# A Fourier, soft-expert and gated layer on one Trainium2 core: the first transform split over 48 rows on the array's quarters, and the row softmax of seven batches moved into the expert loop

## Chip, cores and metric

The kernel runs on one core of a Trainium2 chip. The time is the device time of the whole program in microseconds (us). PE is the matmul engine (TensorE), with its weight loads as PEld; DVE is VectorE, ACT ScalarE, POOL GpSimd, SP the engine that only issues DMAs. Each engine works through its own queue in order. A name with a q behind it (SPq, ACTq) is the queue itself.

## What is computed

```python
def reference(x, w_r, w_i, b_r, b_i, phi, w1, w2, w_gate, w_val, w_out):
    X = rfft(x, axis=1)                        # x: 8 batches, 3072 rows, 256 columns
    Y = soft((X.re + i X.im) @ (w_r + i w_i) + b_r + i b_i)    # shrunk by 0.01 on each part
    x = irfft(Y, n=3072, axis=1).reshape(24576, 256)
    logits = x @ phi                           # 32 slots, 4 for each of 8 experts
    d = softmax(logits, axis=0)                # over all 24576 rows: which rows fill a slot
    slot = relu(d.T @ x, per expert @ w1) @ w2 # 8 experts, 256 to 1024 to 256
    c = softmax(logits, axis=1)                # over the 32 slots of a row
    x = c @ slot
    return (silu(x @ w_gate) * (x @ w_val)) @ w_out            # 256 to 1536 to 256
```

All inputs are float32, the weights of the last layer float64.

## The kernel before

The program has two large parts with a short one between.

**The transform stage** (`phase1`) goes through the 8 batches. The transform of 3072 points is split as 96 x 32. `load_x` (L714) brings a quarter of a batch's columns as `[96, 32, 64]` (for batch 0 `load_first`, L700). `stage_a` (L729) multiplies it by the 96-point table `fwd`: 16 calls a batch, one float32 matmul of 96 rows, 128 outputs and 512 columns each, into one of two PSUM banks that carry the name "ac". VectorE transposes the bank into `chan` (L734). A float32 matmul shows as two records in the trace. `stage_c` (L751) does the 32-point part out of `chan`, also through the two "ac" banks; ScalarE and VectorE split its result into a high and a low part in `xg` and `sg`. `stage_b` (L846) multiplies by the weights, in banks of its own ("pb"), three matmuls to a product. The result is shrunk, collected in `yt`, multiplied by `phi` (`stage_q`, L944) and spread over the partitions by DMAs (L973). From there `logits`, `slots` and `combine` make the softmax over all rows, step by step over the batches, and the softmax over the slots.

`combine` works on a `[96, 32, 32]` tile of logits: maximum of each row (DVE), subtraction (POOL, L1307), exponential (ACT), then sum and reciprocal (`total`, DVE, L1316 to L1318), scaling (`scale`, POOL, L1321), transpose (`turn`, DVE, L1325), a high part (`hi`, ACT, L1330) and a low part (`lo`, POOL, L1334), and a store of both to `c_scr` in DRAM. For the last batch `total` to `store` run in the middle part.

The order of all instructions of this stage is written by a planner (`Plan`). Each job has an engine, a cost (`COST`), a rank and the buffers that it needs; the planner always takes the job that can start first, by rank among equals, and `SHIFT` moves the rank of each kind of job by a fitted number.

**The middle part** (`after_slots`) runs the 8 experts on the slots, loads c of batch 0 (`load_c(0)`, L1685, three DMAs of 384 KB on POOL's queue) and the last layer's weights, and makes the table `gstk` from the slots and the gate weights (`gates`, L1717 to L1720).

**The expert loop** (so called in the diff's words for the gated last layer) has 576 steps, 72 a batch. A step makes two products of c with `gstk` (`gv`, L1733 and L1734), the gate on ACT (L1736), their product on DVE (L1738), and a split into a high and a low part (`split`, ACT L1745, DVE L1746); `mm_out` (L1758) of the step three before then runs six matmuls of 128x128x512. Every 12 steps two banks are transposed by DVE and stored.

Of the kernel before, what the change touches and what calls it, by code (L numbers as in the profile page):

```python
# [10 lines left out]
F32 = mybir.dt.float32  # L11
# [12 lines left out]
R2 = 32  # L24
NCH = 24
# [7 lines left out]
def dft_tables():  # L33
# [7 lines left out]
    n1 = np.arange(R1)  # L41
    n2 = np.arange(R2)
    k2 = np.arange(R2)
    sign = np.where(k2 >= R2 // 2, -1.0, 1.0)
    alt1 = np.where(n1 % 2 == 0, 1.0, -1.0)
    alt2 = np.where(n2 % 2 == 0, 1.0, -1.0)
    k1 = np.array([[j, 23 + j] for j in range(NCH)])
    k1[0] = (0, 47)

    fwd = np.zeros((R1, 4, 32))  # L50
    mix = np.zeros((4, R2, NCH, 2, 2, R2))
    for j in range(NCH):
        for h in range(2):
            if j == 0 and h == 0:
                fwd[:, 0, 0] = 1.0
                fwd[:, 1, 0] = alt1
                for i in range(R2):
                    if i == 0:
                        mix[0, :, j, 0, h, 0] = 1.0
                        continue  # L60
                    src = 0 if i < 16 else 1
                    k = 96 * i if i < 16 else 48 + 96 * (i - 16)
                    a = 2 * np.pi * ((n2 * k) % n) / n
                    mix[src, :, j, 0, h, i] = np.cos(a)
                    mix[src, :, j, 1, h, i] = -np.sin(a)
                continue
            a = 2 * np.pi * ((n1 * k1[j, h]) % R1) / R1
            fwd[:, 2 * h, j] = np.cos(a)
            fwd[:, 2 * h + 1, j] = -np.sin(a)
            a = 2 * np.pi * ((n2[:, None] * (k1[j, h] + 96 * k2)[None, :]) % n) / n  # L70
            mix[2 * h, :, j, 0, h, :] = np.cos(a)
            mix[2 * h + 1, :, j, 0, h, :] = np.sin(a)
            mix[2 * h, :, j, 1, h, :] = -np.sin(a) * sign
            mix[2 * h + 1, :, j, 1, h, :] = np.cos(a) * sign
# [56 lines left out]
    last[0:32, 0] = alt2  # L131
# [3 lines left out]
    def pad(m, rows):  # L135
# [3 lines left out]

    small = np.concatenate(  # L140
        [
            pad(np.concatenate([np.zeros((R1, 8)), fwd.reshape(R1, 128)], 1), R1),
# [17 lines left out]
for _n, _w in (  # L160
# [11 lines left out]
FWD = 136  # L172
# [5 lines left out]
    "load_f": 2.81,  # L178
    "setup_small": -9.39,
    "load_first": -3.7,  # L180
    "stage_a.mm": -28.93,
    "stage_a.turn": 2.94,
    "put": -0.33,
    "free_early": -16.09,
    "load_w": -25.29,
    "mix_w": 3.51,
    "part_w": -17.96,
    "rest_w": -0.28,
    "stage_c.mm": (-12.22, -1.28, -5.52),
    "stage_c.hi": (53.77, -42.32, -55.05),  # L190
    "stage_c.lo": (40.1, 19.86, -25.02),
    "stage_c.one_part": (2.25, -2.27, 4.93),
    "stage_c.add_part": (-68.16, 19.01, -25.95),
    "stage_c.sum_hi": (10.97, 9.66, -13.31),
    "stage_c.sum_lo": (-6.92, -75.37, -42.83),
    "stage_c.last_mm": (36.23, 0.0, 0.0),
    "stage_c.last_out": (-24.98, 0.0, 0.0),
    "stage_b.last_mm": (-10.11, 0.0, 0.0),
    "stage_b.last_out": (3.76, 0.0, 0.0),
    "stage_b.mm": (-0.22, -0.26, -0.14),  # L200
    "after_b.take": (48.09, 1.97, 4.29),
    "after_b.gather": (-37.89, -92.44, -12.86),
    "after_b.relu": (21.51, 7.9, 2.96),
    "after_b.join": (-54.79, -9.98, 9.41),
    "stage_q.mm": (0.0, -9.39, 7.88),
    "stage_q.turn_y": (7.74, 49.03, -2.46),
    "stage_q.turn": (-12.53, -0.89, 4.91),
    "stage_q.spread": (-23.98, -39.91, 59.31),
    "logits.inv_mm": -18.3,
    "logits.sp_mm": -38.62,  # L210
    "logits.sp_out": 26.62,
    "logits.rot": 64.93,
    "logits.join": -32.12,
    "logits.turn": -71.72,
    "logits.l_mm": 44.13,
    "logits.colmax": -29.68,
    "logits.keep_l": 51.42,
    "logits.spread": 15.76,
    "logits.max_mm": 33.28,
    "logits.newmax": 26.07,  # L220
    "logits.factor": 18.59,
    "logits.bc_mm": -2.58,
    "logits.lower": -7.03,
    "logits.expo": -25.93,
    "slots.f_mm": -12.38,
    "slots.turn": 9.73,
    "slots.cross": -27.68,
    "slots.rot": -4.89,
    "slots.join": -8.33,
    "slots.d_mm": -36.49,  # L230
    "slots.evac": -14.41,
    "slots.slot_mm": -32.07,
    "slots.gather": -18.97,
    "combine.rowmax": 14.04,
    "combine.lower": 1.85,
    "combine.expo": -54.13,
    "combine.total": -16.96,
    "combine.scale": -4.82,
    "combine.turn": -12.43,
    "combine.hi": -27.19,  # L240
    "combine.lo": 7.86,
    "combine.store": -22.54,
    "narrow.load": 28.3,
    "narrow.bits": 1.55,
    "narrow.size": 21.04,
    "narrow.value": -7.49,
    "narrow.store": -31.84,
    "load_x": 0.13,
    "narrow.part": 9.87,
    "narrow.rest": 4.99,  # L250
    "stage_q.mm'": (0.0, 0.0, -7.18),
    "stage_q.turn_y'": (0.0, 0.0, 12.3),
    "stage_q.turn'": (0.0, 0.0, 11.0),
    "stage_q.spread'": (0.0, 0.0, -21.67),
    "logits.inv_mm'": -32.46,
    "logits.sp_mm'": -32.14,
    "logits.sp_out'": 25.91,
    "logits.rot'": 31.71,
    "logits.join'": -6.39,
    "logits.turn'": -6.55,  # L260
    "logits.l_mm'": -67.64,
    "logits.colmax'": 60.65,
    "logits.keep_l'": 33.35,
    "logits.spread'": 13.57,
    "logits.max_mm'": -18.0,
    "logits.newmax'": 9.47,
    "logits.factor'": 18.28,
    "logits.bc_mm'": 12.87,
    "logits.lower'": -25.45,
    "logits.expo'": 35.72,  # L270
    "slots.f_mm'": 59.73,
    "slots.turn'": 49.73,
    "slots.cross'": 30.87,
    "slots.rot'": -12.01,
    "slots.join'": 52.75,
    "slots.d_mm'": 12.44,
    "slots.evac'": -2.82,
    "slots.slot_mm'": -78.14,
    "slots.gather'": -22.49,
    "combine.rowmax'": 5.14,  # L280
    "combine.lower'": -35.75,
    "combine.expo'": -34.15,
    "combine.total'": 20.3,
    "combine.scale'": 53.34,
    "combine.turn'": 70.78,
    "combine.hi'": 5.94,
    "combine.lo'": -32.53,
    "combine.store'": 28.18,
    "free_x": -27.72,
    "free_a": 45.67,  # L290
    "free_b": 2.84,
    "fetch_w1": 13.94,
    "fetch_w2": -26.03,
    "fetch_wg": -14.12,
    "hold": 25.89,
# [8 lines left out]
    "stage_a.mm": {"PE": 0.865},  # L304
# [15 lines left out]
    "stage_q.mm": {"PE": 0.56},  # L320
    "stage_q.turn_y": {"DVE": 1.215},
    "stage_q.turn": {"DVE": 0.432},
    "logits.inv_mm": {"PE": 1.32},
# [58 lines left out]
class Plan:  # L382
# [6 lines left out]

    LAG = 0.07  # L390
    HAND, SET, SEEN = 0.65, 0.9, 0.65
    SHY = 0.18

    def __init__(self, shift):
        self.tasks = []
# [111 lines left out]
def kernel(  # L507
# [1084 lines left out]
    def after_slots(ypool, rest):  # L1592
# [65 lines left out]
        for job in rest[0]:  # L1658
            job()
# [162 lines left out]
```

## Time and profile before

| | us |
|---|---|
| median of 3 runs | 1739.52 (1737.23 to 1740.32) |
| the profiled execution: its own time | 1739.96 |
| its span, first to last instruction | 1738.2 |
| PE busy in the span | 1697.5 (98%) |
| VectorE busy | 1283.1 (74%) |
| ScalarE busy | 981.0 (56%) |
| GpSimd busy | 301.2 (17%) |

Busy times are read against the same engine's span. Idle time of an engine that is not the limit costs nothing. The granted clock is that of PE as a share of 2.4 GHz: 1.00 is 2.4 GHz, and a value between 0.5 and 1.00 means that part of the stretch ran at 1.2 GHz.

### The profile page before, as it was taken

The numbers are of one execution on the slowest core, as the hardware profiler recorded it, in microseconds if no ns is written. First come the engines' busy times: TensorE is split into PE (matmuls) and PEld (weight loads), VectorE is DVE, ScalarE is ACT, GpSimd is POOL, SyncE is SP. The second block draws the span as 40 slices with busy tenths as digits, with TensorE's granted clock in tenths as the row PEclk, the third lists the DMA queues.
The fourth block names the chain that finished last, engine by engine and source line by source line (L and its number), as shares of the span: only waits on it lengthen the run. The fifth ranks groups of instructions, "written<-read, shape, count | busy, mean of one in ns | idle before, by whom it ended". The sixth has DMA issues, their size and how long they took to land.

```text
span 1738.2 us, 23243 instructions
## 1 busy us (share of the span) xinstructions
PE 1697.5 (98%) x8266; PEld 1288.5 (74%) x8266; DVE 1283.1 (74%) x2114; ACT 981.0 (56%) x1809; POOL 301.2 (17%) x287
## 2 busy tenths in 40 slices
PE   7999999999999889999999999999999999999998
PEld 4667666676666657888888888888888888888886
DVE  5687978878887536777777777777777777777776
ACT  2565654656556325656656566565565665656654
POOL 1344544445455440000000000000000000000000
PEclk9999999999999999999999999999999999999999
DMA  9557565576545795113112112113112112111111
GB/s 186 97 123 134 128 140 107 138 124 143 136 94 167 232 304 95 25 25 52 24 20 48 23 25 53 25 25 52 25 25 52 25 25 52 25 25 25 25 25 25
DMA packets 258468, 134.44 MB, mean 77 GB/s; under 512 B 209232, under 2 KB 243760, under 8 KB 258352
## 3 DMA queue, kind: packets, MB, share of 16 engines
q1 hardware_dynamic: 248352, 110.14, 31.2%
q0 software_dynamic: 8304, 22.02, 5.5%
q8 instruction: 65, 1.06, 0.3%
q10 hardware_dynamic: 1696, 0.79, 0.2%
q14 instruction: 51, 0.42, 0.1%
HBM read 69.99 MB, written 37.75 MB: 62 GB/s over the span
## 4 chain that ended last, share of the span: by engine, by line
PE 85%; DVE 8%; ACT 2%; DMA 2%; issue 1%; SPq 1%; POOL 0%; DVEq 0%; ACTq 0%; POOLq 0%
PE o L1758 46%; PE pg L1733 8%; PE pb L846 8%; PE pv L1734 8%; PE ac L729 5%; PE ac L751 4%; PE ch L944 1%; PE ch L1015 1%; DVE yt L960 1%; PE ch L1217 1%; PE pb L1578 1%; DVE xg L773 1%; DVE cv L1372 1%; DVE chan L734 1%; DMA x<-in_x_dram 1%
## 5 line engine op out<-in xcount | busy, mean ns | idle before, releaser
L1758 PE MATMUL o<-hh,wo 128*128 128x512 f32 x2304 | 722.5, 395 | 0.0
L1738 DVE TENSOR_TENSOR h<-sg,pv 128x512 f32<-128x512 f32 x576 | 394.3, 685 | 275.5 <-ACT sg L1736 274.1
L1736 ACT ACTIVATE sg<-pg 128x512 f32<-128x512 f32 x576 | 344.6, 598 | 426.1 <-PE pg L1733 426.1
L1758 PEld LDWEIGHTS o<-hh,wo 128*128 128x128 f32 x2304 | 434.3, 188 | 100.7
L1758 PE MATMUL o<-hl,wo 128*128 128x512 f32 x1152 | 453.8, 394 | 0.0
L1746 DVE TENSOR_TENSOR hl<-h,hh 128x512 fp32r<-128x512 f32 x576 | 393.9, 684 | 0.1
L1745 ACT ACTIVATE hh<-h 128x512 fp32r<-128x512 f32 x576 | 359.4, 624 | 0.2 <-DVE h L1738 0.2
L1758 PEld LDWEIGHTS o<-hl,wo 128*128 128x128 f32 x1152 | 216.1, 188 | 51.9
L1733 PE MATMUL pg<-cst,gstk 96*128 96x512 f32 x576 | 228.9, 397 | 3.4 <-DMA cst<-c_scr 3.4
L1734 PE MATMUL pv<-cst,gstk 96*128 96x512 f32 x576 | 226.6, 393 | 0.7 <-DVE gstk L1720 0.7
L918 POOL TENSOR_TENSOR yt<-r,yt 128x512 f32<-128x512 f32 x96 | 126.6, 1319 | 207.4 <-ACT yt L909 121.8
L1685 POOL DMA_DIRECT2D cst<-c_scr x24 | 13.4, 565 | 803.4 <-PE pv L1734 797.4
L846 PE MATMUL pb<-xg,wh 128*128 128x512 f32 x384 | 140.6, 447 | 3.3 <-ACT yt L899 2.1
L1734 PEld LDWEIGHTS pv<-cst,gstk 96*128 96x128 f32 x576 | 110.0, 191 | 26.6 <-DVE gstk L1720 1.4
L1733 PEld LDWEIGHTS pg<-cst,gstk 96*128 96x128 f32 x576 | 108.3, 188 | 28.7 <-issue 4.6
L729 PE MATMUL ac<-xq,fwd 96*128 96x512 f32 x224 | 111.8, 612 | 3.9 <-DVE chan L734 3.4
L751 PEld LDWEIGHTS ac<-cm,chan 128*128 128x128 f32 x768 | 97.5, 196 | 15.7 <-issue 6.9
L734 DVE STREAM_TRANSPOSE chan<-ac 128x512 f32<-128x512 f32 x128 | 88.4, 702 | 25.7 <-PE ac L729 22.7
L751 PE MATMUL ac<-cm,chan 128*128 128x128 f32 x768 | 104.5, 286 | 1.7 <-DVE xg L773 1.3
L846 PEld LDWEIGHTS pb<-xg,wh 128*128 128x128 f32 x384 | 66.1, 189 | 41.9 <-issue 17.3
L770 ACT ACTIVATE xg<-ac 128x512 fp32r<-128x512 f32 x96 | 56.6, 595 | 47.5 <-PE ac L751 45.7
L792 POOL TENSOR_TENSOR sg<-sf,sg 128x256 fp32r<-128x256 f32 x96 | 70.2, 745 | 68.0 <-ACT sg L788 56.1
(145 smaller groups left out, 1590.0 us busy)
## 6 DMA issues: line engine op xcount, KB each, us to landing
out_dram<-ob SPq DMA_DIRECT2D x190, 128.0 KB, 2.8
yi<-yt SPq DMA_DIRECT2D x376, 64.0 KB, 2.1
xq<-in_x_dram SPq DMA_DIRECT2D x28, 768.0 KB, 8.2
cst<-c_scr POOLq DMA_DIRECT2D x24, 384.0 KB, 6.2
w1s<-in_moe_w_dram POOLq DMA_DIRECT2D x8, 1024.0 KB, 9.2
w2s<-in_moe_w_dram SPq DMA_DIRECT2D x7, 1024.0 KB, 11.3
x<-in_x_dram SPq DMA_DIRECT2D x4, 768.0 KB, 12.0
cvi<-in_moe_w_gate_dram SPq DMA_DIRECT2D x6, 512.0 KB, 5.9
```

Source lines behind the costliest of these rows:

```text
L729: nc.tensor.matmul(out=pt, lhsT=fwd[:, 8 - 8 * dh:136 - 8 * dh], rhs=T[kq][:, :, d1:d1 + 16], start=True, stop=True)
L734: nc.vector.transpose(out=chan[:, 12 * dh:12 * dh + 16, d0:d0 + 16, :].rearrange("p j d i -> p d j i"), in_=T[ka].rearrange("p n d -> p d n"),
L751: nc.tensor.matmul(out=pt[:, :, q:q + 2, i // 2, :], lhsT=chan[:, 16 * dh + j // 2, :, j % 2], rhs=cm[:, j, :].rearrange("p (c h k) -> p c ...
L846: nc.tensor.matmul(out=pt, lhsT=w[:, dh, m, es], rhs=xx, start=m != 1 and dh == 0 and n == 0, stop=dh == 1 and n == 2, skip_group_check=True,)
L918: e.tensor_sub(out=part(), in0=quarters(T[kr]), in1=part())
L1733: nc.tensor.matmul(out=pg, lhsT=gstk[:, 0, f * 128:(f + 1) * 128], rhs=rhs, start=True, stop=True)
L1734: nc.tensor.matmul(out=pv, lhsT=gstk[:, 1, f * 128:(f + 1) * 128], rhs=rhs, start=True, stop=True)
L1736: nc.scalar.activation(out=sg, in_=pg, func=AF.Silu)
L1738: nc.vector.tensor_mul(out=h, in0=sg, in1=pv)
L1745: nc.scalar.activation(out=hh, in_=h, func=AF.Copy)
L1746: nc.vector.tensor_sub(out=hl, in0=h, in1=hh.bitcast(F32))
L1758: nc.tensor.matmul(out=po_t[0][k], lhsT=w[:, f % 4, k * 128:(k + 1) * 128], rhs=a, start=(f == 0 and m == 0), stop=(f == NF - 1 and m == 2 ...
```

## The change

The first transform takes 48 points where it took 96: even and odd rows of x (c = 0, 1) are transformed apart, with the same 48-point table, and the combination of the two is put into the table `mix` of the second transform, whose size stays. A matmul then has 48 rows and 64 outputs, a quarter of the array. The table stands twice in `fwd`, at partitions 0 and 64.

- Batches 1 to 7: a tile of x holds one parity: 64 columns at partitions 0 to 47 and the next 64 at partitions 64 to 111. Each half is a DMA, one on SP's queue and one on ACT's. Three such tiles are kept where two were. `stage_a` runs 8 times a batch and issues four matmuls into both "ac" banks: rows 0 or 64 into bank 0 or 1, parity 0 or 1 into outputs 0 to 63 or 64 to 127. Two transposes follow.
- Batch 0: `load_first` loads rows of 128 columns (512 bytes) and not 64, in two DMAs for each half of the columns, on the two queues; `stage_a0` runs 16 times with two matmuls into the two halves of one bank. The small table is loaded ahead of everything.
- `combine` for batches 1 to 7 ends with the exponential, which is stored to `e_scr`. The rest runs in the expert loop, in pieces of a quarter, during the batch before the one that needs it.
- c is loaded in three tiles a batch, 128 KB for each DMA; of batch 0 only the first is loaded where all was.
- The late two of the last `yi` DMAs a part go from ACT's queue to POOL's.
- The planner's costs are set anew in places, its choice gets a small term of the rank, and all numbers of `SHIFT` are new.

```diff
-        def load_x(b, dq):
+        def half_x(k, r):
+            _, b, dh, c = k
+            d0 = 128 * dh + 64 * r
+            (nc.sync, nc.scalar)[r].dma_start(
+                out=T[k][64 * r:64 * r + R0],
+                in_=x[b, :, d0:d0 + 64].rearrange("(p n c) d -> c p n d", n=R2, c=2)[c],
+            )
...
+        def stage_a0(dh, dd, rank):
...
+                pt = bank(ka, [128, R2, 16], "ac")
+                for r in range(2):
+                    rows = slice(64 * r, 64 * r + R0)
+                    nc.tensor.matmul(
+                        out=pt[64 * r:64 * r + 64], lhsT=fwd[rows, 8 - 8 * dh:72 - 8 * dh],
+                        rhs=T["x0", dh][rows, :, 16 * dd:16 * dd + 16], start=True, stop=True, skip_group_check=True,
+                    )
...
-                nc.tensor.matmul(
-                    out=pt, lhsT=fwd[:, 8 - 8 * dh:136 - 8 * dh], rhs=T[kq][:, :, d1:d1 + 16], start=True, stop=True
-                )
+                pt = [bank(k, [128, R2, 16], "ac") for k in ka]
+                for r, c in ((0, 0), (1, 1), (0, 1), (1, 0)):
+                    rows = slice(64 * r, 64 * r + R0)
+                    nc.tensor.matmul(
+                        out=pt[r][64 * c:64 * c + 64], lhsT=fwd[rows, 8 - 8 * dh:72 - 8 * dh],
+                        rhs=T[kq[c]][rows, :, d1:d1 + 16], start=True, stop=True, skip_group_check=True,
+                    )
...
-            if b == B - 1:
-                return (total, scale), (turn, hi, lo, store(chi, 0), store(clo, 1))
+            if b:
+                add("SP", 0.06, k + 0.2, keep, r=[ls], w=[("es", b)], bus=1.1)
+                return
...
-        def load_c(b):
-            t = cp.tile([R1, 3, 1024], F32R, tag="cst", name="cst")
+        def load_c(b, q):
+            cst_t[b, q] = t = cp.tile([R1, 1024], F32R, tag=f"cst{q}", name="cst")
             for r, s in ((0, 0), (1, 0), (2, 1)):
...
+                nc.gpsimd.dma_start(out=t[32 * r:32 * r + 32], in_=c_scr[b, s, 32 * q:32 * q + 32])
...
+            jobs = {2: [load], 15: [norm], 44: [store]}
+            for i in range(4):
+                k = slice(8 * i, 8 * i + 8)
+                for at, f in ((8, total), (17, scale), (25, turn), (26, high), (33, low)):
+                    jobs.setdefault(at + 2 * i, []).append(lambda f=f, k=k: f(k))
+            for q in range(3):
+                jobs[50 + 4 * q] = [lambda q=q: load_c(b, q)]
```

The keys of `jobs` are the steps of a batch at whose end a piece is issued; `rest_c(b + 1)` is spread over the steps of batch b.

## Rows read from the trace of the kernel before

**Rows 1.** Windows: span, busy time (records) of PE, PEld, DVE, ACT, POOL, clock, DMA.
```profile
650.00:660.00 10.00, 8.63 (x16) 4.47 (x17) 3.65 (x6) 3.97 (x8) 1.13 (x2) 0.66 1.78 330
660.00:1738.00 1078.00, 1071.80 (x4609) 867.99 (x4608) 795.21 (x1247) 642.19 (x1149) 10.02 (x18) 1.00 0.19 31
```
**Rows 2.** Windows: seven stretches of 75 us from 45 to 570 us, summed.
```profile
sum 525.00, PE 512.83 PEld 347.66 DVE 425.18 ACT 300.71 POOL 248.88; mean PE 73.26 PEld 49.67 DVE 60.74 ACT 42.96 POOL 35.55
```
**Rows 3.** Waits of PE, 40 to 620 us: total us, times, longest.
```profile
PE ac L729 <- DVE chan L734: 3.4, 11, 0.4
```
**Rows 4.** Timeline of PE: start, us, line, operation, out<-in, count.
```profile
127.57 1.88 PE L729 MATMUL ac<-xq,fwd 96*128 96x512 f32 x4
129.39 0.64 PE L944 MATMUL ch<-yt,phis 128*32 128x256 f32 x8
...
586.55 0.62 PE L846 MATMUL pb<-sg,wh 128*128 128x512 f32 x2
587.01 0.40 PE L846 MATMUL pb<-sg,wl 128*128 128x512 f32 x1
...
588.66 0.40 PE L846 MATMUL pb<-xg,wl 128*128 128x512 f32 x1
588.98 0.64 PE L944 MATMUL ch<-yt,phis 128*32 128x256 f32 x8
589.55 0.73 PE L846 MATMUL pb<-xg,wh 128*128 128x512 f32 x2
...
624.88 3.64 PE L1626 MATMUL ph<-w1s,tail 128*32 128x512 f32 x32
```
**Rows 5.** Instructions grouped by line, whole span: busy us, mean ns, idle before.
```profile
L1746 DVE TENSOR_TENSOR hl<-h,hh 128x512 fp32r<-128x512 f32 x576 | 393.9, 684 | 0.1
...
L1334 POOL TENSOR_TENSOR ls<-vt,td 96x1024 fp32r<-96x1024 f32 x8 | 19.0, 2372 | 21.7 <-ACT td L1330 21.7
...
L1321 POOL TENSOR_TENSOR ls<-ls,rs 96x1024 f32<-96x1024 f32 x8 | 15.6, 1953 | 7.7 <-DVE rs L1318 7.2 <-PE pb L846 0.5
...
L1325 DVE STREAM_TRANSPOSE vt<-ls 96x1024 f32<-96x1024 f32 x8 | 9.8, 1219 | 0.4 <-PE ch L1223 0.4
...
L1316 DVE TENSOR_REDUCE rs<-ls 96x32 f32<-96x1024 f32 x8 | 9.5, 1185 | 0.8 <-ACT ls L1312 0.7
...
L1317 DVE TENSOR_SCALAR rs<-rs 96x32 f32<-96x32 f32 x8 | 4.3, 540 | 0.3
...
L1318 DVE RECIPROCAL rs<-rs 96x32 f32<-96x32 f32 x8 | 2.8, 349 | 0.3
```
**Rows 6.** One line's instructions (L973) on ACT's queue: ns least, median, most.
```profile
L973 ACTq DMA_DIRECT2D yi<-yt x8: 592/614/1001, 596.5 to 602.4; - x8
```
**Rows 7.** Timeline of the first 60 us.
```profile
3.27 13.06 SPq L700 DMA_DIRECT2D x<-in_x_dram  x4
...
10.83 13.61 PE L729 MATMUL ac<-x,fwd 96*128 96x512 f32 x24 [10.83 <-DMA x<-in_x_dram]
...
19.74 1.58 DVE L734 STREAM_TRANSPOSE chan<-ac 128x512 f32<-128x512 f32 x2 [0.36 <-PE ac L729]
...
21.67 1.58 DVE L734 STREAM_TRANSPOSE chan<-ac 128x512 f32<-128x512 f32 x2 [0.36 <-PE ac L729]
```
**Rows 8.** Windows with loads of 256-byte rows, then of 4 KB rows.
```profile
8.00:16.00 8.00, 5.17 (x7) 2.18 (x8) 1.57 (x3) 0.34 (x1) 3.10 (x3) 1.00 1.39 169
24.50:27.50 3.00, 2.86 (x6) 1.07 (x7) 2.12 (x3) 0.00 (x0) 0.00 (x0) 1.00 1.04 401
```
**Rows 9.** Timeline from the middle part into the expert loop.
```profile
643.61 3.70 PE L1717 MATMUL pg<-wg,tail 128*128 128x512 f32 x8 [0.52 <-DVE tail L1703]
...
647.97 0.68 DVE L1720 TENSOR_TENSOR gstk<-pg,gstk 32x512 fp32r<-32x512 f32 x1 [1.03 <-ACT gstk L1719]
...
650.66 0.76 PE L1733 MATMUL pg<-cst,gstk 96*128 96x512 f32 x1 [3.35 <-DMA cst<-c_scr]
...
652.50 5.81 PE L1717 MATMUL pg<-wg,tail 128*128 128x512 f32 x8
```

More of the change, by code (lines that the diff above doesn't have):

```diff
@@ L24 @@
 R2 = 32
+R0 = 48
 NCH = 24
@@ L45, in dft_tables, with put_mix @@
     alt1 = np.where(n1 % 2 == 0, 1.0, -1.0)
+    alt0 = np.where(m1 % 2 == 0, 1.0, -1.0)
     alt2 = np.where(n2 % 2 == 0, 1.0, -1.0)
[L47 to L51, printed above, removed]
-    for j in range(NCH):
+    k1 = np.array([[j, 48 + j] for j in range(NCH)])
+    k1[0] = (0, 24)
+    fwd = np.zeros((R0, 2, 32))
+    mix = np.zeros((2, 2, R2, NCH, 2, 2, R2))
+    def put_mix(part, j, c, h, i, v):
+        mix[:, part, :, j, c, h, i] = v.reshape((R2, 2) + v.shape[1:]).swapaxes(0, 1)
@@ L53, in dft_tables @@
+    every = slice(None)
+    for j in range(NCH):
+        if j == 0:
+            fwd[:, 0, 0] = 1.0
+            fwd[:, 1, 0] = alt0
+        else:
+            a = 2 * np.pi * ((m1 * j) % R0) / R0
+            fwd[:, 0, j] = np.cos(a)
+            fwd[:, 1, j] = -np.sin(a)
         for h in range(2):
             if j == 0 and h == 0:
[L55 to L61, printed above, removed]
+                put_mix(0, j, 0, h, 0, np.ones(2 * R2))
+                for i in range(1, R2):
@@ L243 @@
[L243 to L259, printed above, removed]
@@ new lines @@
+    "combine.scale": 58.16,
+    "combine.turn": 8.98,
+    "combine.hi": -22.27,
+    "combine.lo": -27.85,
+    "combine.store": -45.58,
+    "narrow.load": -52.99,
+    "narrow.bits": 317.51,
+    "narrow.size": 0.94,
+    "narrow.value": 160.14,
+    "narrow.store": 5.64,
+    "load_x": 94.72,
+    "load_x2": 227.84,
+    "narrow.part": 90.74,
+    "narrow.rest": 31.14,
+    "stage_q.mm'": (-2.79, -15.17, 313.51),
+    "stage_q.turn_y'": (107.70, -63.80, 70.44),
+    "stage_q.turn'": (-73.65, 26.48, 53.60),
@@ L466, in run @@
                 t = tasks[i]
-                slot = set()
+                slot, more = set(), {}
                 for name, _ in t["new"]:
-                    row, n = rings[name], self.bufs[name]
+                    row, n = rings[name], self.bufs[name] - more.get(name, 0)
+                    more[name] = more.get(name, 0) + 1
                     if len(row) >= n:
@@ new lines, in turn, with go @@
+            def turn(r):
+                def go():
+                    d0 = 64 * r + d1
+                    nc.vector.transpose(
+                        out=chan[:, 12 * dh:12 * dh + 16, d0:d0 + 16, :].rearrange("p j d i -> p d j i"),
+                        in_=T[ka[r]].rearrange("p n d -> p d n"),
+                    )
+                return go
+            add(
+                "PE", 1.2, rank, mm, r=["f", kt] + [(*k, r) for k in kq for r in range(2)], w=ka,
+                new=[("ac", k) for k in ka] + ([("tt", kt)] if dd == 0 else []),
+            )
@@ L742, in stage_c @@
+            for r in range(2):
+                add("DVE", 0.6, rank, turn(r), r=[ka[r]], w=[(*kt, ps[r])])
         def stage_c(b, g, hb, dh, rank):
```

404 lines of the change are left out of this document (230 added, 174 removed), and 2 rows, old and new, of the table add.

## Prediction

> **What bounds the kernel now.** I first read the table of windows for each stage. In the expert loop the matmul engine is busy 1071.8 us of 1078 [rows 1]: this loop runs at the pace of PE, about 1078 / 576 = 1.87 us a step. In the seven stretches of the transform stage from 45 to 570 us, PE is busy 512.83 of 525 us (98%), VectorE 425.18 (81%), ScalarE 300.71, GpSimd 248.88 [rows 2]. So the transform stage too is set by PE, and VectorE is next. Then the waits of PE in that stage: the longest that concerns the first transform is 3.4 us in all, for the transposes that empty its two banks [rows 3]. A microsecond of PE work taken out of this stage is therefore worth most of a microsecond, until VectorE or the exchange between PE and VectorE becomes the limit.
>
> **The change, part by part.**
>
> *First transform of batches 1 to 7.* Before, a batch has 16 calls of one 96x128x512 float32 matmul. Afterwards it has 8 calls (pairs) of four 48x64x512 matmuls, one on each quarter of the array, 56 pairs in all. What two old calls cost: the four records that start at 127.57 are followed by the next group at 129.39, so 1.82 us [rows 4]; I use 1.80. What four quarters cost is in no row, because no matmul before uses the array's row halves apart. The nearest rows are column quarters: 16 matmuls of 128x32x512 (32 records) take 3.64 us, so 0.91 us for four [rows 4]. There four small matmuls cost what one large one does. Such a group standing alone pays for its surroundings: the group of four 128x32x256 starts 0.32 us after the matmul ahead of it (588.66 to 588.98) where two ordinary ones take 0.46 us (586.55 to 587.01), 0.23 each, so 0.09 on the way in; and the next one starts 0.57 after it (588.98 to 589.55) where half of 0.91 is 0.455, so 0.115 on the way out [rows 4]. Together 0.2. A pair then costs 0.91 + 0.2 = 1.1 us, and 56 x (1.80 - 1.10) = 39 us less work on PE. Bounds: with no cost for switching 56 x (1.82 - 0.91) = 51; if the row halves run one after the other, a pair costs 2 x 0.91 + 0.2 = 2.0 and the change adds 56 x 0.2 = 11.
>
> *The two banks.* A pair takes both banks of "ac" at once. Before, PE filled one while VectorE emptied the other. Now the next pair, or a block of the second transform, can only begin when its bank has been emptied; two such transposes take 1.58 us [rows 7], 0.79 each. PE has other work in other banks (the products with the weights above all), and the order is planned so that this fills the gap. If nothing filled it, one transpose a pair would show: 56 x 0.79 = 44 us, more than the gain. If all is filled, nothing. The nearest row is the present wait for the same transposes, 3.4 us in 11 times [rows 3], so I take somewhat under a fifth of it, 8 us.
>
> *The row softmax of batches 1 to 7.* Sum, reciprocal, scaling, transpose and the two splits leave the transform stage: VectorE loses (9.5 + 4.3 + 2.8 + 9.8) / 8 = 3.3 us a batch, GpSimd (15.6 + 19.0) / 8 = 4.3 [rows 5]. Neither is the limit there, so this is worth nothing by itself. It keeps VectorE behind PE: per 75 us it has 425.18 / 7 = 60.7, then 57.4 against PE's 73.3 - 5.6 = 67.7, which is 85% where it was 83% [rows 2, 5].
>
> *The same work in the expert loop.* There a batch has 72 steps of 1.87 us. The two VectorE instructions of a step, of one size, take 2 x 0.684 = 1.37 [rows 5], which leaves 0.5 us a step, some 36 us a batch. The new work is 3.3 us of VectorE in nine pieces, the largest 0.54 + 0.35 = 0.9, and 4.3 us of GpSimd in eight pieces. A piece of 0.9 is late by 0.4 us, made good in the next step. PE takes the products of the step three before, so a delay below one step (1.87 us) reaches nothing. I cost it at nothing; without this cover the price is 0.4 us x 9 x 7 = 25 us. ScalarE, 1.2 us a step, has room. The loads of c are in nine pieces a batch and not three, on GpSimd's queue, which has nothing else to do but these pieces; they are issued from step 50 and wanted at step 72, 41 us later.
>
> *x on two queues.* Each tile of x is two DMAs, one on ScalarE's queue: four a batch, 28 in all, and two at the start. A DMA issue on that queue took 0.61 us [rows 6], so 2.4 us a batch on an engine that is busy 43 of 75 us [rows 2]. What is queued behind them is the copies out of PSUM. ScalarE would also stand still if a tile of x is not free yet. I take nothing for this by itself and count it in the second rival.
>
> *The start.* Now the four loads of x block their queue for 13.06 us, the first matmul runs at 10.83, and from then on the transposes set the pace, two in 1.94 us [rows 7]. Rows of 256 bytes move 169 GB/s, rows of 4 KB 401 [rows 8], and the new rows of 512 bytes lie between. The first block needs twice the bytes (1.57 MB): at 169 GB/s 9.3 us after the queue starts, at twice that 4.7. The load of the small table now goes first, so x starts some 2 us earlier. First matmul between 8 and 12, so -3 to +1. The preparation of w, some 1.7 us of VectorE, now falls between the transposes. I take -1.
>
> *The way into the expert loop.* The first product with c waited for it from 647.97 + 0.68 = 648.65 to 650.66 [rows 9]. All three parts of c were loaded ahead of it. Now only one part is, and neither the last batch's splits nor its stores stand in front. That is -2.0. PE idled there, the granted clock over 650 to 660 us is 0.66 [rows 1], so part of it ran at 1.2 and not 2.4 GHz, and eight records of the gates took 5.81 us where the same eight took 3.70 before the gap [rows 9]. That is -2.1 if the gap goes. Together -4, at least 0 if the weights are late instead.
>
> Sum, against the profiled execution's own 1739.96 us (0.4 above the median of the three runs): 1740 - 39 + 8 - 1 - 4 = 1704.
>
> **A rule that speaks against it.** In batch 0 the two matmuls of a call take different row halves and write halves of the same bank. No row shows two row halves in one bank; four column quarters in one bank run together at 0.91 us [rows 4]. The Trainium skill, TensorEngine Tiling (Array Packing), section Restrictions and Gotchas, says that different row tiles cannot access one PSUM bank at the same time. No run so far shows this. It is the third rival below.
>
> **The rivals.** *Row halves one after the other (slower).* A pair costs 2.0 (above): +11. The 16 calls of batch 0 cost 2.0 where the transposes now set 0.97: +16. 1740 + 11 + 16 - 5 = 1762. For it: no row shows row halves together. Against it: column quarters do run together, at the full gain. Without batch 0 it decides from a pair of 1.80 + 5/56 = 1.9 us.
>
> *The gain is lost to waits.* The bank exchange shows in six of ten pairs, 24 us, and ScalarE's queue stops now and then for x, say a quarter of the 28 x 0.61, 4 us: 1740 - 39 + 28 - 5 = 1724. For it: the bank is now taken in one piece. Against it: PE waits for transposes 3.4 us today [rows 3], and VectorE keeps its margin.
>
> *Batch 0 serialised by its shared bank*, 16 x (2.0 - 0.97) = 16: 1720.
>
> *The expert loop is disturbed.* 25 us as above: 1704 + 25 = 1729. Against it: the margin of a whole step.
>
> *More than I count.* All exchange hidden and a pair at 1.0: 1740 - 45 - 5 = 1690.
>
> **How the numbers follow.** Likeliest (1704, own range 1695 to 1714): 0.55. Lost to waits: 0.16. Batch 0: 0.05. Loop disturbed: 0.06. More: 0.12. Row halves in series: 0.06. The range reaches from 1688, just below the best case, to 1727, which leaves out part of the disturbed loop and the slower case, and some of each tail, about 2 in 10. All cases but the last lie more than 0.2% (3.5 us, what a measurement can tell from no change) below 1739.5. Between the lost gain and the slower case lies a small chance of about the same time. Faster 0.91, same 0.03, slower 0.06.
>
> **What would show it.** In the trace after: four groups of two records of the first transform that start within some tens of ns, and about 1.1 us from a pair's start to the next other matmul. The stage before the last logits should end some 35 us earlier. PE's wait for the transposes should be near 10 us. The first product with c should start within about 1 us of the last write of the gate table `gstk`, with no drop of the granted clock around it. The expert loop should last 1078 us within 2. Wrong would be: records of the two row halves 0.4 us apart; waits of PE for transposes of 20 us and more; gaps of PE inside the expert loop at steps 14 to 39 of each batch.

## The result, and the profile after

The changed kernel takes 1761.11 us (median of 4 runs, 1758.33 to 1762.39) against 1739.23 for the kernel before on the same chip: a ratio of 1.0125, 95% interval 1.0107 to 1.0142. It is slower by 22 us; the prediction had it faster by 36. The profiled execution took 1762.39 us, its span is 1760.6.

I cut both spans at three marks that each trace has: the first matmul of the second transform (`stage_c`), the first of `hold`, with which the middle part opens, and the first product with c. The rows of windows between them, of the kernel before (span, busy time and records of PE, PEld, DVE, ACT, POOL, then the granted clock, the DMA share and GB/s):

```profile
28.48:590.35 561.87, 544.91 (x3107) 372.55 (x3106) 446.74 (x765) 319.06 (x628) 265.69 (x240) 0.99 0.62 136
590.35:650.66 60.31, 54.69 (x506) 37.69 (x505) 24.07 (x73) 12.81 (x21) 19.90 (x18) 1.00 0.83 254
650.66:1738.20 1087.54, 1080.44 (x4624) 872.43 (x4624) 798.87 (x1252) 646.16 (x1156) 11.15 (x20) 1.00 0.20 34
```

The same of the kernel after, and the sum of its seven windows of 75 us, which answers to [rows 2]:

```profile
35.32:616.25 580.93, 531.82 (x3331) 350.46 (x3329) 419.81 (x744) 316.78 (x624) 235.58 (x226) 0.96 0.77 123
616.25:674.70 58.45, 55.35 (x510) 38.11 (x506) 21.28 (x69) 9.80 (x17) 19.70 (x26) 1.00 0.98 298
674.70:1760.60 1085.90, 1077.72 (x4625) 871.02 (x4624) 822.51 (x1323) 655.40 (x1185) 84.89 (x128) 1.00 0.21 41
...
sum 525.00, PE 481.10 PEld 313.83 DVE 381.95 ACT 280.55 POOL 205.77; mean PE 68.73 PEld 44.83 DVE 54.56 ACT 40.08 POOL 29.40
```

The loss stands in three places: the start is 35.32 - 28.48 = 6.8 us longer; in the transform stage PE has 544.91 - 531.82 = 13.1 us less work, but it idles 580.93 - 531.82 = 49.1 us where it idled 17.0, which is 32.1 more; the middle part and the expert loop give back 1.9 and 1.6. Together 6.8 - 13.1 + 32.1 - 1.9 - 1.6 = 22.3. So the stage is no longer set by PE: 481 of 525 us, not 513. What it waits for is in the list of PE's waits from 40 to 620 us (total us, times, longest), which answers to [rows 3]:

```profile
PE ac L792 <- DMA xq<-in_x_dram: 19.6, 5, 6.2
PE pb L918 <- ACT r L981: 9.6, 8, 1.3
PE pb L918 <- ACT yt L971: 7.2, 4, 4.3
PE pb L918 <- DVE yt L974: 5.0, 1, 5.0
...
PE ac L792 <- DVE chan L800: 0.7, 1, 0.7
```

As a wait of PE the exchange of the two banks, for which the prediction set 8 us, is the last row alone: 0.7. A part of it counts as busy time, because PE is still at the first quarter when the others are held up. One such pair in the timeline:

```profile
212.72 1.87 PE L792 MATMUL ac<-xq,fwd 48*64 48x512 f32 x8
212.98 0.42 DVE L851 TENSOR_TENSOR sf<-ac,sf 128x256 f32<-128x256 f32 x1 [0.51 <-ACT sf L848]
...
213.48 0.23 PEld L792 LDWEIGHTS ac<-xq,fwd 48*64 48x64 f32 x6 [0.57 <-issue]
```

It takes 1.87 us where most pairs take 1.09: the weights of three of its quarters are loaded only at 213.48, just after VectorE's last read of an "ac" bank (212.98 + 0.42 = 213.40). Eight of the 56 pairs are stretched like this, by 5.5 us together.

The first row of the waits is x, which the kernel before never waited for after its start. The timeline shows one such wait, first the DMA issues on the two queues, then PE (start, us, engine, line, operation):

```profile
300.24 1.48 SPq L741 DMA_DIRECT2D xq<-in_x_dram  x2
...
306.07 0.57 ACTq L741 DMA_DIRECT2D xq<-in_x_dram  x1
306.95 1.50 ACTq L741 DMA_DIRECT2D xq<-in_x_dram  x1
```

```profile
312.32 1.07 PE L792 MATMUL ac<-xq,fwd 48*64 48x512 f32 x2
318.25 1.98 PE L792 MATMUL ac<-xq,fwd 48*64 48x512 f32 x6 [4.85 <-DMA xq<-in_x_dram]
320.15 1.22 PE L918 MATMUL pb<-xg,wh 128*128 128x512 f32 x2
...
326.73 1.09 PE L792 MATMUL ac<-xq,fwd 48*64 48x512 f32 x8
327.75 0.73 PE L918 MATMUL pb<-xg,wh 128*128 128x512 f32 x2
```

The two halves of one tile are issued 6 us apart, on SP's queue at 300.24 and on ScalarE's at 306.07. In each of the five waits PE starts with the half that is there and stops for the other. After the gap the clock is down (granted 0.50 from 318.20 to 321.60): the pair takes 1.98 us for six records and two products 1.22, where below they take 1.09 for eight and 0.73. The granted clock of the stage is 0.96 and not 0.99.

The two queues' rows in the list of DMA issues (KB each, median us to landing); before, one whole tile of 768 KB landed in 8.2:

```profile
xq<-in_x_dram SPq DMA_DIRECT2D x28, 384.0 KB, 9.1
xq<-in_x_dram ACTq DMA_DIRECT2D x28, 384.0 KB, 10.0
```

The start, against [rows 7, 8]: SP's queue, the first matmuls, and the window of 8 to 16 us:

```profile
1.19 1.73 SPq L725 DMA_DIRECT2D x<-in_x_dram  x2
2.96 10.26 SPq L1511 DMA_DIRECT2D wst<-in_w_r_dram  x1
```

```profile
15.55 8.51 PE L766 MATMUL ac<-x,fwd 48*64 48x512 f32 x24 [15.55 <-DMA x<-in_x_dram]
25.82 9.54 PE L766 MATMUL ac<-x,fwd 48*64 48x512 f32 x40 [1.75 <-DVE chan L772]
```

```profile
8.00:16.00 8.00, 0.45 (x2) 0.32 (x4) 0.00 (x0) 0.00 (x0) 0.00 (x0) 1.00 1.20 181
```

and the issues of x for batch 0 (KB each, median us to landing):

```profile
x<-in_x_dram ACTq DMA_DIRECT2D x2, 768.0 KB, 14.4
x<-in_x_dram SPq DMA_DIRECT2D x2, 768.0 KB, 17.1
```

The first matmul comes at 15.55 us and not at 10.83. Rows of 512 bytes move 181 GB/s, hardly more than the 169 of rows of 256, and the first block now needs twice the bytes, one DMA of each queue. The four landings took 9.7 to 20.0 us: ScalarE's first half was there at 10.4, SP's only at 15.5. Behind x the load of w blocks the queue for 10.26 us.

The way into the loop, against [rows 9]:

```profile
673.95 0.68 DVE L1795 TENSOR_TENSOR gstk<-pg,gstk 32x512 fp32r<-32x512 f32 x1 [2.70 <-ACT gstk L1794]
...
674.69 0.55 PE L1806 MATMUL pg<-cst,gstk 96*128 96x512 f32 x1
```

The first product starts 0.06 us after the table is written (673.95 + 0.68 = 674.63), as forecast, and the clock stays up (1.00 in both windows above).

### The profile page after: what moved, and what is told of

Read it like the earlier page. It is cut to its first block, busy times and chain, and to the rows that moved or that the text cites. A ratio compares the mean times of both kernels' runs of the same rounds, so it can differ in the third digit from the quotient of the medians.

```text
span 1760.6 us, 23950 instructions
## 1 busy us (share of the span) xinstructions
PE 1682.9 (96%) x8522; PEld 1263.9 (72%) x8522; DVE 1276.8 (73%) x2160; ACT 984.9 (56%) x1830; POOL 344.7 (20%) x388
## 4 chain that ended last, share of the span: by engine, by line
PE 86%; DMA 6%; DVE 3%; ACT 2%; SPq 2%; issue 1%; POOL 0%; ACTq 0%; DVEq 0%; POOLq 0%
PE o L1831 46%; PE pb L918 10%; PE pg L1806 8%; PE pv L1807 8%; PE ac L823 3%; PE ac L792 3%; DMA xq<-in_x_dram 3%; PE ch L1289 1%; DMA cvi<-in_moe_w_gate_dram 1%; PE ch L1016 1%; PE ch L1087 1%; PE ch L1341 1%; DVE xg L845 1%; ACT xg L842 1%; PE ch L1153 1%; PE pb L1658 1%
## 5 line engine op out<-in xcount | busy, mean ns | idle before, releaser
L990 POOL TENSOR_TENSOR yt<-r,yt 128x512 f32<-128x512 f32 x93 | 120.5, 1295 | 187.2 <-ACT yt L981 118.9
L1867 POOL TENSOR_TENSOR e<-e,rs 96x256 f32<-96x256 f32 x28 | 22.7, 834 | 506.4 <-DVE rs L1864 506.4
L800 DVE STREAM_TRANSPOSE chan<-ac 128x512 f32<-128x512 f32 x112 | 73.7, 691 | 49.5 <-PE ac L792 49.5
L792 PE MATMUL ac<-xq,fwd 48*64 48x512 f32 x448 | 76.1, 645 | 20.4 <-DMA xq<-in_x_dram 19.6
L918 PE MATMUL pb<-sg,wh 128*128 128x512 f32 x192 | 68.9, 442 | 14.0 <-ACT r L981 8.9
```

What stands on the lines that cost most here:

```text
L792: nc.tensor.matmul(out=pt[r][64 * c:64 * c + 64], lhsT=fwd[rows, 8 - 8 * dh:72 - 8 * dh], rhs=T[kq[c]][rows, :, d1:d1 + 16], start=True, s ...
L800: nc.vector.transpose(out=chan[:, 12 * dh:12 * dh + 16, d0:d0 + 16, :].rearrange("p j d i -> p d j i"), in_=T[ka[r]].rearrange("p n d -> p ...
L918: nc.tensor.matmul(out=pt, lhsT=w[:, dh, m, es], rhs=xx, start=m != 1 and dh == 0 and n == 0, stop=dh == 1 and n == 2, skip_group_check=True,)
L990: e.tensor_sub(out=part(), in0=quarters(T[kr]), in1=part())
```

## The experiments

Where one run was made, its time stands against 1739 to 1742 us of the kernel before, measured beside it; where more were made, the median is given with the ratio and its interval. "Start" below is the mark of the second transform.

**Why is x late? Loads alone, and three changes of the second half.** The theories were the row stride (every second row is loaded), ScalarE's queue as such, and DMAs to 48 partitions being slow. One kernel only loads: 1.57 MB in eight forms, one after the other.

> Only loads of x, one form after the other, 1.57 MB each time, three rounds; the computation is left out and the output is not written but for 128 rows. Forms: xa whole rows in one DMA on SP's queue as before; xb every second row, halves at partitions 0 and 64, all on SP's queue; xc the same on two queues, as in the changed kernel; xd two queues, consecutive rows; xe two queues, the two halves of a tile of opposite parity; xf one queue, consecutive rows; xg 512-byte rows by parity on two queues as in batch 0 now; xh 512-byte whole rows on one queue. In the changed kernel packets of 256 bytes took longer than before. Theory S (reading every second row slows the DRAM side): xb and xc some 14 us, xa, xd, xe, xf some 10 us. Theory Q (two queues disturb each other): xc, xd, xe some 14 us, xa, xb, xf some 10. Theory P (48 partitions at a time are the slow part): all of xb to xf some 14, xa 10.

Its timeline, in the first of three rounds, of the form as before (xa: whole tiles of 96 partitions on SP's queue), as 48-partition halves on one queue (xb), and as halves on two queues (xc); a VectorE copy marks each landing:

```profile
0.73 3.53 SPq L578 DMA_DIRECT2D xa<-in_x_dram  x2
...
11.00 0.15 DVE L557 COPY acc<-xa 96x1 f32<-96x1 f32 x1 [3.25 <-DMA xa<-in_x_dram]
11.18 0.57 SPq L585 DMA_DIRECT2D xb<-in_x_dram  x1
...
25.01 0.15 DVE L557 COPY acc<-xb 48x1 f32<-48x1 f32 x1 [2.22 <-DMA xb<-in_x_dram]
25.19 1.44 SPq L594 DMA_DIRECT2D xc<-in_x_dram  x2
...
36.98 0.15 DVE L557 COPY acc<-xc 48x1 f32<-48x1 f32 x1 [0.65 <-DMA xc<-in_x_dram]
```

The same bytes take 10.3 us whole, 13.8 as halves on one queue, 11.8 as halves on two. Consecutive rows in place of every second one took 13.3 (one queue) and 12.2 (two), 512-byte rows 10.5 (halves, two queues) and 10.4 (whole); the other rounds lie within 0.6 us of these. So the stride is not it, the second queue helps, the halves cost 15 to 35%, and longer rows gain 1.3 us as halves and nothing as whole tiles. The Trainium skill, SBUF — State Buffer, section Door 1: The DMA port swizzle (why `[64,N]` ≈ `[32,N]`), has a transfer's rate go by how many of 16 ports its partitions reach, and partitions 0 to 63 reach half of them. The direction agrees (1.57 MB / 13.8 us = 114 GB/s against 153); the full factor of two isn't seen here. Its section "Can I just issue two DMAs to hit both halves?" gives +6% for two at once; here it was 13.8 / 11.8, +17%.

In the kernel itself, each a small change of `half_x` (given in short):

```diff
# e_contig      - "(p n c) d -> c p n d"   + "(c p n) d -> c p n d"     (consecutive rows)
# e_one_queue   - (nc.sync, nc.scalar)[r]  + (nc.sync, nc.sync)[r]
# e_opposite    - [c]                      + [c ^ r]                    (and T[kq[c ^ r]] in the matmul)
```

> The changed kernel, but for batches 1 to 7 the halves of x are read as 1536 consecutive rows in place of every second one, so that the transform is of other data; all else stays. Theory S: the loads land as early as the order assumes, PE's 19.6 us of waits for x and the 6.8 us at half clock behind each go, the time falls by 25 to 45 us to some 1725. Theories Q and P: no change, 1761 within 4.

> The changed kernel, but both halves of x for batches 1 to 7 go on SP's queue, at the places in the order where they were. Theory Q: faster by 20 us or more. Theories S and P: the same or a little slower, 1758 to 1775, since the half that was ScalarE's now stands behind the spread of yi on SP's queue.

> The changed kernel, but a tile of x holds one parity in its first half and the other in its second, so that the two DMAs that run together read odd and even rows; the matmuls take their halves accordingly. If reading one parity alone is slow because only every second kilobyte of DRAM is touched (theory S), this brings back most of e_contig's gain: 1725 to 1740. If the stride as such is slow, or under theories Q and P: 1761 within 4.

1761.81, 1758.11 and 1759.31 us; PE's wait for x stays at 19.0, 19.8 and 17.9. None of the three is the cause of that wait.

**Is the second half issued late?** In the planner the tile is placed by `load_x`, and `load_x2` follows it as a later user of the same tile, behind its planned landing. The edit issues both at once, with the offsets untouched:

```diff
 def load_x(k): ...
     half_x(k, 0)
+    half_x(k, 1)
 def load_x2(k): ...
-    half_x(k, 1)
+    pass
```

> The changed kernel, but both halves of a tile of x for batches 1 to 7 are issued where the first one was, one on each queue; the job that issued the second half does nothing, and no other instruction moves. In the trace of the changed kernel the second halves are issued some 6 us after the first ones, about when those land, and PE waits 19.6 us for them. Theory L (the second half is late because the planner lets it start only after the first has landed): PE's waits for x fall under 5 us, the half clock behind them goes, and the time falls by 20 to 35 us, to 1726 to 1741. Theory P (the loads of 48 partitions are slow in themselves, wherever they are issued): the waits stay above 12 us, 1750 to 1761.

1744.52 us, 16.6 less (20 to 35 were expected): the late issue alone is most of the 22 us. PE no longer waits for x; its longest waits, and the window between the marks:

```profile
PE pb L919 <- ACT r L982: 9.6, 8, 1.3
PE ac L793 <- DVE chan L801: 8.0, 5, 3.5
```

```profile
38.75:598.29 559.54, 524.61 (x3331) 345.94 (x3330) 420.35 (x744) 315.86 (x624) 237.62 (x226) 0.98 0.71 127
```

The same 3331 records take 7.2 us less than after, at a clock of 0.98, and the idle time is 34.9 and not 49.1. The wait for `chan` (8.0) comes from what stands ahead of the transposes in VectorE's queue:

```profile
294.70 0.89 SPq L1439 DMA_DIRECT2D cvi<-in_moe_w_val_dram  x1
...
306.39 0.43 DVE L1447 TENSOR_SCALAR cv<-cvi 128x512 int32<-128x512 int32 x1 [4.73 <-DMA cvi<-in_moe_w_val_dram]
...
308.19 1.31 DVE L801 STREAM_TRANSPOSE chan<-ac 128x512 f32<-128x512 f32 x2
```

VectorE stands for expert weights (`cvi`), whose load was issued on SP's queue behind two halves of x (289.12); the transposes come after. Such waits of VectorE sum to 18.6 us here, to 27.9 with both halves on SP's queue (next), to 10.2 with whole loads (e_whole_cvi, below), and to none in the kernel before.

Three variants. Both halves on SP's queue (`nc.sync` in `half_x`, on top of the edit above):

> As e_early, with both halves on SP's queue. Theory L: like e_early within 5 us, since the queue doesn't matter. If ScalarE's time for issuing costs anything, this is faster than e_early by up to 10 us; if one queue moves the halves more slowly, it is slower by as much.

1755.23: one queue is 11 us worse. The planner told of both (a job of its own places the tile, both loads follow it, and the order is planned anew):

```diff
+ add("SP", 0.01, t, place_x(k), w=[(*k, 2)], new=("xq", k))
- add("SP", 0.06, t, load_x(k), w=[(*k, 0)], new=("xq", k), bus=2.2)
+ add("SP", 0.06, t, load_x(k), w=[(*k, 0)], bus=2.2)
```

> The changed kernel with one thing told to the planner otherwise: the tile's place is a job of its own, both loads come after it and not one after the other, and both have the same rank. The whole order is made anew, with offsets that were fitted to the other one. Theory L: no second half is issued more than 2 us behind its first, waits for x under 5 us, 1725 to 1745; the offsets no longer fit, which can cost some us. Theory P: 1750 or more.

1766.81, a miss: x's wait falls to 5.3, but another order comes out of the fitted offsets (that of `load_x2` was set to `load_x`'s), with 14.0 us for ScalarE's `r`. The third loads batch 0 in 64-column pieces as well:

> As e_early, and batch 0's loads are cut into pieces of 64 columns, so that the first four calls need half the bytes. The first matmul of the changed kernel waited 15.6 us for x. If that wait is for the 1.57 MB that the first call needs: first matmul at 9 to 11 us and 4 to 6 us faster than e_early. If it is for something else: as e_early.

1754.28: the first matmul comes at 11.3, but then VectorE stands in `mix_w` for w, which is loaded behind x, and PE waits 17.9 us for a transpose.

**The start.** w first, then batch 0's x in 64-column pieces (`for d in (0, 64)` around the DMA in `load_first`, the w loads moved into `load_f`), with and without the early second half:

> As e_early_first, and the loads of w_r, w_i and the biases are issued ahead of all of x, as before the change, and not behind the first batch. In e_early_first VectorE waited for w between two transposes of batch 0 and PE 17.9 us for VectorE. If the start is made of that wait and of the first load: the second transform begins near 30 us where it was 38.8 in e_early and 28.5 before the change, and the time is 8 to 10 us under e_early's 1744.5, 1734 to 1738, a little under the kernel before. If the start doesn't matter because what follows waits for loads anyway: 1742 to 1746.

> The changed kernel with the start of e_start alone; the second halves of x stay where the change put them. If the two effects add: 1761 less 5 to 8 us, 1752 to 1757, with the waits for x of 19 us still there. If the late halves hide what the start gains: 1761 within 3.

1749.91 (ratio 1.0050, 1.0033 to 1.0066) and 1769.76. Both missed: the first matmul is at 16.6. ScalarE's queue brings its four pieces ahead, while SP's queue is still at w. Two more, both with the early second half: all of batches 0 and 1 on SP's queue (e_start2), and w and x dealt evenly over both, with the first expert weights ahead of batch 1's x (e_start3):

> Both halves of x are issued together, the weights come first, batch 0's x comes in 64-column pieces all on SyncE's queue in the order of need, and batch 1's pieces follow on that queue too, so that nothing on ScalarE's queue runs ahead. Theory start (the remaining loss over the kernel before is mostly the first 40 us): first matmul at 10 to 12 us, the second transform starts at about 30 instead of 38.8, and the time is 1734 to 1739. Theory halves (the remaining loss is in the slower landing of 48-partition halves all along the transforms): the early start is eaten by the first waits for x, and the time stays at 1742 to 1748.

> The whole computation. Both halves of x are issued together; each of the two queues brings one of the two weight matrices first and then its half of batch 0's x in 64-column pieces, and the first load of expert weights goes ahead of batch 1's x on SyncE's queue. Theory start: first matmul at about 10 us, the second transform starts at 27 to 31 instead of 38.8, no wait for the first expert weights, and the time is 1732 to 1738, below the kernel before. Theory halves: the queues are full of 48-partition packets, the loads behind them come late, and the time stays at 1742 to 1750.

1753.31 (1.0072, 1.0055 to 1.0088) and 1748.31 (1.0046, 1.0032 to 1.0060). The first shows what one queue costs; its window of 8 to 16 us:

```profile
8.00:16.00 8.00, 4.56 (x8) 1.03 (x8) 0.62 (x1) 0.00 (x0) 0.00 (x0) 1.00 1.40 109
```

48-partition loads on one queue move 109 GB/s where whole ones moved 169 [rows 8]. Its first matmul is the earliest, at 9.9, but the first expert weights stand behind batch 1's x on the same queue: VectorE waits 15.6 us for them, and PE 14.2 for VectorE. In all four the second transform starts at 37 to 41 us.

**The price of the halves in the kernel before.** `load_x` there cuts each tile of batches 1 to 7 in two DMAs of 48 partitions, both on SP's queue:

> The kernel before, but each load of x for batches 1 to 7 is cut into two DMAs of 48 partitions, both on SP's queue and at the same place. In the loads alone such halves took 13.1 us for 1.57 MB where whole ones took 10.3. Theory P (slow 48-partition loads are what costs): PE waits for x appear, and the time rises by 10 us or more. Theory L: within 4 us of before.

1747.22, 6.7 us slower in one run, between what the two theories expected. PE waits for x only 1.0 us. By the marks, 1.2 us of it are in the start, 2.9 in the transform stage, 4.4 in the middle part, and -1.2 in the loop. So halves cost something in the kernel before too, but not through PE's wait for x, and how is not shown.

**The change with whole loads.** From batch 1 on one DMA brings consecutive rows to 96 partitions, as before; the array's quarters read them (rows are not sorted by parity, so the first transform is another one, with the same matmuls). The first attempt gave the second row group 32 rows in place of 48:

```diff
+ nc.sync.dma_start(out=T[k][0:96], in_=x[b, :, q0:q0 + 64].rearrange("(p n) d -> p n d", n=R2))
- rows = slice(64 * r, 64 * r + R0)
+ rows = slice(64 * r, 64 * r + (R0, 32)[r])
```

> As the kernel with both halves issued together, but from batch 1 on each quarter batch of x is one DMA of consecutive rows to 96 partitions, as in the kernel before; the second row group multiplies 32 of its 48 rows only, and rows are not sorted into the two halves, so part of the first transform is left out; the matmuls keep their number and their columns. Theory halves: x is no longer late, no half-clock stretches after waits for x, and from the second transform's first matmul to the first one of the state the time falls from 559 to below 545 us; total 1725 to 1735. Theory start: that stretch stays at 555 to 560 and the total at 1742 to 1747. Both: the first with the start still 10 us late.

2015.73 us: it answered another question. The group of the first transform, and one pair in the timeline:

```profile
L798 PE MATMUL ac<-xq,fwd 48*64 48x512 f32 x448 | 297.4, 777 | 0.0
```

```profile
315.02 4.88 PE L798 MATMUL ac<-xq,fwd 48*64 48x512 f32 x8
319.84 1.22 PE L924 MATMUL pb<-xg,wh 128*128 128x512 f32 x2
```

With 48 rows in one group and 32 in the other the pair takes 4.88 us and not 1.09, about 1 us for each of the first three and 1.8 for the last: they run one after the other. That is worse than the prediction's slower rival (2.0 a pair), in a case that the change itself avoids. The clock falls too, to 0.78 over 45 to 570 us, and the two products behind this pair take 1.22.

With 48 rows in both groups (16 of the second hold zeros, in three tiles that are kept):

> As the kernel with both halves issued together, but from batch 1 on each quarter batch of x is one DMA of consecutive rows to 96 partitions on SyncE's queue; the matmuls keep their two groups of 48 rows, of which 16 of the second group hold zeros, and the rows are not sorted into halves, so the first transform is not the right one. Theory halves: x is not late, and from the second transform's first matmul to the first one of the state the time falls from 559 to below 548 us; total 1728 to 1735. Theory start: that stretch stays at 555 to 560 and the total at 1742 to 1747.

1728.64 (0.9931, 0.9916 to 0.9947). With batch 0 whole as well, behind w, as before:

> As e_whole2, with batch 0's x too in four whole DMAs of 64 columns on SyncE's queue, behind the weights, as in the kernel before (the first transform is again not the right one). Theory halves and start together: first matmul at about 11 us, the second transform starts at 26 to 30, and the total is 1710 to 1722, so that nearly all of the forecast gain is there when x comes as it came before. If the change has a loss of its own that has nothing to do with how x is loaded, the total stays above 1730.

1729.83 (0.9937, 0.9920 to 0.9953). The second transform now starts at 28.8 and not 36.7, and nothing comes of it (1710 to 1722 was expected). Its timeline says where it went:

```profile
46.64 0.43 DVE L1462 TENSOR_SCALAR cv<-cvi 128x512 int32<-128x512 int32 x1 [8.63 <-DMA cvi<-in_moe_w_gate_dram]
...
49.17 1.22 PE L934 MATMUL pb<-sg,wh 128*128 128x512 f32 x2 [7.26 <-DVE yt L990]
```

VectorE waits for the first expert weights, whose load stands behind three tiles of x on SP's queue, where there were two before (the change keeps three). The last two runs issue that load ahead of batch 1's x, with whole loads and in the kernel that computes everything (e_early's edit):

```diff
 def load_x(k): ...
+    first_cvi()          # in short: narrow's load for i == 0, issued here
     sb(xpool, k, [64 + R0, R2, 64], "xq", 3)
```

> As e_whole3 (x in whole DMAs of 96 partitions, so that the first transform is not the right one), with the first load of expert weights issued ahead of batch 1's x. If the wait for these weights is what ate the earlier start, TensorE's 7.3-us gap at 42 us goes and the time falls from 1729.8 to 1722 to 1725. If the earlier start is lost for another reason (the order of the work after it), it stays at 1728 to 1731.

> The whole computation: both halves of x issued together, and the first load of expert weights ahead of batch 1's x. If the waits for those weights count, 1.4 to 5 us below 1744.5, so 1739 to 1743, level with the kernel before. If not, 1743 to 1746.

1721.78 (0.9886, 0.9870 to 0.9902) and 1743.49 (10 runs; 1.0010, 1.0000 to 1.0019). The first is what the change is worth when x comes in whole loads and the first expert weights ahead of it: 19 us, and 10 without the latter (1729.83). The kernel before with these weights moved ahead was not run. The windows of the first between the marks:

```profile
28.92:574.56 545.64, 518.19 (x3331) 344.50 (x3329) 421.16 (x744) 316.21 (x624) 238.26 (x226) 0.99 0.63 133
574.56:632.00 57.44, 54.33 (x507) 37.84 (x504) 20.61 (x68) 9.54 (x17) 19.69 (x26) 1.00 1.00 305
632.00:1719.10 1087.10, 1078.76 (x4628) 871.37 (x4626) 823.71 (x1324) 655.36 (x1186) 84.93 (x128) 1.00 0.21 41
```

The second is the best version that computes everything: level with the kernel before within the 0.2% that can be told. No version here that computes everything is faster than the kernel before.

## Why the prediction was wrong

Its frame held: the stage was set by PE, and the change takes work off PE. It failed at **x on two queues**, which it costed at nothing by itself, looking at ScalarE's issue time alone and not at when each half is issued and how fast it lands. From the run with whole loads (span 1719.1) to the changed kernel (1760.6) lie 41.5 us: 6.4 in the start (28.92 to 35.32), 21.7 in idle time (545.64 - 518.19 = 27.4 to 49.1), 13.6 in PE's time for the same records (518.19 to 531.82, the clock at 0.96), -0.2 behind. By the single edits, medians: 16.6 of it by the late issue of the second half (1761.1 to 1744.5), 21.7 by the halves themselves and the start that goes with them (1743.5 to 1721.8); the place of the first expert weights is worth 8 with whole loads (1729.8 to 1721.8) and 1 with halves, less than these runs can tell. Of the 21.7, the two traces (spans 1736.3 and 1719.1, 17.2 apart) have 11.1 in the start (second transform at 40.04 and at 28.92) and 6.3 in the stage.

*First transform, -39.* The matmuls came out as forecast: where nothing holds it up, a pair takes 1.02 us to the next start (326.73 to 327.75), and nowhere do the two row groups of 48 run in series. But with whole loads PE's time between the marks falls by 544.91 - 518.19 = 26.7, 12 less than forecast. Here is the way out of a group of quarters, in the rows of the weight loads; after:

```profile
326.73 0.21 PEld L792 LDWEIGHTS ac<-xq,fwd 48*64 48x64 f32 x8 [0.36 <-DVE acc L1360]
327.75 0.30 PEld L918 LDWEIGHTS pb<-xg,wh 128*128 128x128 f32 x2 [0.81 <-issue]
```

and before:

```profile
212.07 0.30 PEld L729 LDWEIGHTS ac<-xq,fwd 96*128 96x128 f32 x2
212.62 0.19 PEld L846 LDWEIGHTS pb<-sg,wh 128*128 128x128 f32 x1 [0.24 <-issue]
```

After L729 the next weights load while the matmul still runs (its two records take from 212.18 to 213.20). After the quarters the load begins only when they are through, and the first product ends 0.43 us behind them, where another one adds 0.23. Counted in the timeline, 46 of the 56 pairs have a product with the weights right behind them: 46 x 0.2 = 9 us. The new order also leaves groups of 32 outputs for such a product 42 times instead of 24, 18 x 0.2 = 4. Together 13. The prediction had this price at 0.115 a group, read from a smaller group [rows 4], so 56 x 0.115 = 6 of it was in its sum already, and it had not counted the other groups. That leaves 7 of the 12; about as much again is time in which a pair waits for its second bank (next paragraph). Summed by the ends of the records, the two traces agree: the quarters take 40.2 us less than the old records (105.6 to 65.4, with 7.2 of bank waits in it), the products with the weights 16.3 more (212.9 to 229.3), the rest 2.8 less.

*Two banks, +8.* Near in size, and the reason is the one named, though it mostly shows as PE's busy time and not as a wait. With whole loads 11 of the 56 pairs start three of their quarters 0.4 to 0.8 us behind the first, each time 0.05 to 0.11 us after VectorE ends an instruction, in all 11 a transpose or another read of an "ac" bank. That is 7.2 us. PE's waits for the transposes are 2.7 there, and 3.4 before. The idle time grows by 27.45 - 16.96 = 10.5, and for this the sum had no term: PE waits for ScalarE's `r` (eight times 1.2 us, none before) and `yt` (8.2 us, 2.1 before). Why ScalarE is late there was not tried. (In the rival "lost to waits", six of ten pairs would have been 34 x 0.79 = 27 us, not 24.)

*The start, -1.* +6.8. The bound "twice the rate" for 512-byte rows was wrong (181 against 169 GB/s; by themselves 10.4 against 10.3 us whole, 10.5 against 11.8 as halves on two queues), the first block has twice the bytes, and its two halves landed 5 us apart. With whole loads it is +0.4.

*Row softmax and expert loop, 0; way into the loop, -4.* Right: the loop is 1.6 us shorter, with no gap for the new pieces, and the middle part 1.9: together 3.5.

*Rivals.* Row halves in series gave nearly the measured time, 1762, but by chance, since its mechanism is not there: a pair of batches 1 to 7 takes 1.09 us, and L766, batch 0 in one shared bank, runs 8.51 + 9.54 = 18.1 us where 16 calls in series would take 16 x 2.0 = 32. So the rule weighed in the prediction (the Trainium skill, TensorEngine Tiling (Array Packing), Restrictions and Gotchas) costs nothing that shows here. "Lost to waits" came nearest: it named ScalarE's queue, at 4 us, but as a standstill of ScalarE and not as a late x; the waits for x came to 19.6 with the clock on top. The loss by late loads had no rival with a price of its own, though the DMA share was at 0.62 of the stage and the tiles of x landed after 8.2 us.

## What to carry to other kernels

When a transfer is cut in two, price each half: when its issue comes up in its queue's order, and how fast it lands; here two 48-partition halves took 11.8 to 13.8 us where the whole took 10.3, and halves issued 6 us late cost 16.6 us of the kernel. Look also at what stands behind such a load in its queue: VectorE's waits for expert weights grew from none to 18.6 us. In a stage that is 98% PE a late load is paid twice, as the gap and as the lower clock after it. And small matmuls on parts of the array save their own time, but the next full-array matmul pays 0.2 us; putting such groups side by side would save some of that (not tried here).

## What the runs showed of the hardware beyond that

- Quarters of 48 rows and 64 outputs run together, four in 1.02 us. In batch 0, two that use different row groups and write halves of one bank run together as well (ten calls of two in 9.54 us). With 48 rows in one group and 32 in the other they ran one after the other, 4.88 us.
- After the gap of 4.85 us the granted clock was 0.50 for 3.4 us (318.20 to 321.60), which is 1.2 GHz and not 2.4: products came 0.43 us apart (321.17 to 321.60) and not 0.23. Over the whole stage it is 0.96.
- As whole tiles 512-byte rows landed no faster than 256-byte rows (10.4 and 10.3 us for 1.57 MB); as halves on two queues they took 10.5 us and not 11.8.
- The two DMAs of x were issued in 1.73 us, and the small load of w behind them then took 10.26 us to issue: what a queue holds already can delay the issue of the next load. What sets this amount wasn't tried.
